# Expert slots of 384 tokens in place of 256, in the routed second layer of an attention and mixture kernel

## The chip, the core and the metric

The kernel runs on one core of a Trainium2 chip. Its engines work side by side, each through its own list of instructions in order: PE (TensorE, matrix products), DVE (VectorE) and ACT (ScalarE) for work on elements, POOL (GpSimd) for small work and for transfers whose addresses are computed on the chip, SP (SyncE) for the other transfers. They meet at semaphores. Matrix products land in PSUM, eight banks of 2 KB a partition, and ACT or DVE must read them out before a bank is used again. The metric is the device time of one execution in microseconds (us); runs of the same kernel are summed up by their median.

## The reference

Three stages follow each other. Windowed attention (4 sequences of 576, 8 heads of 64, each position sees the 64 up to itself) gives 2304 tokens of 512. A dense layer multiplies by `w_in` (512 x 2048), applies a clipped square and multiplies by `w_out`. A routed layer then sends each token to one of eight experts:

```python
logits = x @ w_gate + modality_bias[modality_id]
e_idx = np.argmax(logits, axis=1)
...
gate_w = probs[np.arange(N), e_idx]
for e in range(E):
    mask = e_idx == e
    h = np.maximum(x[mask] @ w1[e], 0.0)          # 512 -> 1024
    out[mask] = gate_w[mask, None] * (h @ w2[e])  # 1024 -> 512
```

With the inputs of the reference two experts get all tokens: 1136 and 1168 of 2304.

## The kernel before

**Precision by parts.** Every product of the dense and routed layers is made of three matrix products: each operand is split into a rounded part (made by ACT) and the rest (made by DVE), and high x high, low x high and high x low are added in PSUM. So a weight that is loaded costs an ACT cast and a DVE subtraction before PE can use it.

**The first two stages** go through the tokens in six chunks of 384 (`CT`). For each of 16 slices `f` of the hidden width, `l1` makes a tile of 128 x 384 with 12 matrix products (line 445), ACT and DVE turn it into two operands, and `l2` adds it into three banks of 128 x 512 (line 483). Attention of the next chunk is woven in. `route` (line 514) takes the logits of a finished chunk, picks experts, and scatters each token's number into tables by slot position (line 591). After the fourth chunk `order` puts the slots that are sure to be full in front, so that the first `EARLY` slots can begin before the last chunk is routed. `final` (line 663) ends the routing and writes the table `meta`, from which the later slots read their expert and their place.

**The routed layer** is a loop over `NS0` = 10 slots (lines 1071 to 1089). A slot is up to 256 (`SL`) tokens of one expert; a row of `SL` per slot is computed whether filled or not. Nine slots are whole; the tenth is a half slot (`half_slot`) of 128. Further slots stand under `tc.If(used > i)` and run only if the routing needs them.

- `gather` (line 748) runs on POOL: it reads the slot's token numbers and fetches the tokens, 128 at a time, from the stored output of the dense layer. `prep_half` (line 774) transposes 128 of them on PE (line 777) and splits them into `zh` and `zl` (ACT line 779, DVE line 780).
- `slot` (line 782), first layer: four PSUM tiles `hp` of 128 x 512, each holding two slices of 256 columns; 24 matrix products of 256 columns fill one (line 791). ACT writes the rounded relu (line 799), DVE the rest (line 800). Two PSUM buffers alternate, so a tile has to be read out while the next is filled.
- `l2_slot`, second layer: for each 128 tokens 24 matrix products of 512 columns (line 814), a scaled copy by ACT (line 821) and a scatter to the output by POOL (line 822).
- `wsteps` loads the expert weights of coming slots, 16 pieces of 256 KB a slot (line 722 on SP's queue), and splits each (ACT line 727, DVE line 728). Four buffers hold raw pieces, so the load of one begins when the piece four before it has been split. The table `PS` says how many of these steps stand behind each step of a slot: 3, 3, 3, 3 behind the four tiles of the first layer, then 2, 1, 1, 0.
- `advance` takes a step of the last chunk's `route`.

SP's order is that of the source throughout. ACT's is from the end of the dense layer on, and PE's from the third slot on. Elsewhere a scheduler of the language sets the order when the program is built.

Of the kernel before, what the change touches and what calls it, by code (L numbers as in the profile page):

```python
# [9 lines left out]
F32 = mybir.dt.float32  # L10
F32R = mybir.dt.float32r
# [6 lines left out]
P = 128  # L18
B, H, S, D = 4, 8, 576, 64
NT = B * S  # L20
# [50 lines left out]
def moe_kernel(ctx, tc, qT, kT, v, w_in, w_out, mod, wg, wgT, mbias, w1, w2, cst, tri, empty, out, spec):  # L71
# [113 lines left out]
        G.memset(t, 0.0)  # L185
        return t

    prod = tile_of([P, DM], "prod")
    wgb = []
    LGB = 4  # L190
    run = state([P, E], "run")
# [322 lines left out]
    def route(c):  # L514
# [16 lines left out]
        if c < NC - 1:  # L531
            store()
            lg = tile_of([P, TT, E], f"lgd{c}", tag="r_lg")
            for t in range(TT):
                for e in range(E):
                    V.tensor_tensor_reduce(  # L536
                        prod, yt[t], wgb[0][:, e, :], 1.0, 0.0, ALU.mult, ALU.add, lg[:, t, e : e + 1]
                    )
                    if e % LGB == LGB - 1:
                        yield  # L540
        else:
            lg = yield from pe_logits(c, yt)
            store()
# [74 lines left out]
            yield from final()  # L618

    def by_position(dst, vec, name):  # L620
        t = tile_of([P, NS, NS], name, tag="u", bufs=2)
        V.tensor_tensor(t, eqk, bc(vec, 1, NS), op=ALU.mult)
        V.tensor_reduce(dst, t, axis=AX.X, op=ALU.add)

# [120 lines left out]
    def w2s(i, f, lo):  # L745
        return piece(i % 2, (2 + lo) * NP + f)

    def gather(i, rows=NT, halves=2):
        rr = G.value_load(meta[0:1, 0 if i < KNOWN else 2, i : i + 1], min_val=0, max_val=(NS - 1) * SL)
        rt = tile_of([P, TT, 2, 2], f"rt{i}", tag="rt", bufs=2)  # L750
        for t in range(TT):
            G.dma_start(rt[:, t], tabs[t][bass.ds(rr, SL), :].rearrange("(h p) w -> p h w", p=P))
        rc = tile_of([P, 2, 2], f"rc{i}", tag="rc", bufs=4)
        oi = tile_of([P, 2], f"oi{i}", I32, tag="oi", bufs=4)
        gi = tile_of([P, 2], f"gi{i}", I32, tag="gi", bufs=4)
        gf = tile_of([P, 2], f"gf{i}", tag="gf", bufs=4)
# [12 lines left out]
        return g, oi, rc  # L769
# [37 lines left out]
    def l2_slot(i, g, t, mid):  # L807
        hh, hl = hid[0], hid[1]
        yo = ps.tile([P, DM], F32, tag=f"y{(2 * i + t) % TT}", name=f"yo{i}_{t}", bufs=1)
        n = 0  # L810
        sl = slice(t * P, (t + 1) * P)
        for f in range(NF2):
            for a, b in ((hh, 0), (hh, 1), (hl, 0)):
                T.matmul(yo, a[:, f, sl], w2s(i, f, b), start=n == 0, stop=n == 3 * NF2 - 1)  # L814
# [12 lines left out]

    def half_slot(i, g, x, mid):
        hh, hl = hid[0], hid[1]
        xh, xl = x  # L830
        sl = slice(0, HS)

        def l1(fp):
            hp = ps.tile([P, 2, P], F32, tag="h", name=f"hp{i}_{fp}", bufs=2)
            w = [experts[1, lo * NP // 2 + fp].rearrange("p (q k n) -> p k q n", q=2, k=KD) for lo in range(2)]
            n = 0
            for k in range(KD):
                for a, b in ((xh, 0), (xl, 0), (xh, 1)):
                    T.matmul(hp, a[:, k, sl], w[b][:, k], start=n == 0, stop=n == 3 * KD - 1)
                    n += 1  # L840
            r = tile_of([P, 2, P], f"hr{i}_{fp}", tag="y", bufs=4)
            A.activation(r, hp, AF.Relu)
            return r

        def turn(fp, r):
            rt = aux([P, 2, P], f"rt{i}_{fp}")
            for u in range(2):
                T.transpose(rt[:, u, :], r[:, u, :], C["ident"])
            fs = slice(2 * fp, 2 * fp + 2)
            A.copy(hh[:, fs, sl], rt)  # L850
            V.tensor_tensor(hl[:, fs, sl], rt, hh[:, fs, sl].bitcast(F32), op=ALU.subtract)
# [9 lines left out]
        yield from l2_slot(i, g, 0, mid)  # L861

    man = ExitStack()
    ET = mybir.EngineType
# [130 lines left out]
    for n in range(len(its) + LAG):  # L995
# [49 lines left out]
        if c == NC - 1 and f == 6:  # L1045
            ws = wsteps(0, NS0)
            eg = [gather(i, (NC - 1) * CT) for i in range(2)]
            ex = new_x2(0)
        if c == NC - 1 and f >= 9:
            for _ in range(2 if f < 11 or f == NF - 1 else 3):  # L1050
                next(ws)
                ndone += 1
            if f in (10, 11):
                prep_half(0, f - 10, eg[0], ex)
# [5 lines left out]
    hm = tile_of([P, 2, NF2, SL], "hm", F32R, tag="dec")  # L1060
    hid = [hm[:, 0], hm[:, 1]]
    gq = dict(enumerate(eg))
    gq[2] = gather(2, (NC - 1) * CT)
    x = ex
    PS = (3, 3, 3, 3, 2, 1, 1, 0)

    def advance():
        if rts and next(rts[0], "end") == "end":
            rts.clear()

    for i in range(NS0):
        if i == NS0 - 3:
            used = nc.values_load(nused[0:1, 0:1], min_val=1, max_val=NS + 1)  # L1073
        if i == 2:
            m2.enter_context(tc.manual_schedule(engines={ET.PE}))
        nx = new_x2(i + 1) if i + 1 < NS0 else None
        for n, _ in enumerate((slot if i + 1 < NS0 else half_slot)(i, gq[i], x, advance)):
            advance()
            for _ in range(PS[n]):
                next(ws, None)  # L1080
            if i == 0 and n == 3:
                gq[3] = gather(3, (NC - 1) * CT)
            if n == GN and EARLY <= i + GP < NS0:
                assert not rts
                gq[i + GP] = gather(i + GP, halves=2 if i + GP + 1 < NS0 else 1)
# [8 lines left out]
    for i in range(NS0, NS + 1):  # L1094
        ifs.enter_context(tc.If(used > i))
        g = gather(i)
        x = new_x2(i)
        for _ in wsteps(i, i + 1):
            pass
        for h in range(2):  # L1100
            prep_half(i, h, g, x)
        for _ in slot(i, g, x, lambda: None):
            pass
# [47 lines left out]
```

## Time and profile before

| | us |
|---|---|
| median of 3 runs (lowest, highest) | 747.73 (744.97, 749.30) |
| the profiled execution, its own time | 745.43 |
| its span from first to last instruction | 743.7 |
| PE busy in it | 731.2 |
| routed layer: first product to the half slot's start | 501.3 to 722.9 |
| half slot and last output | 722.9 to 743.7 |

All times in the rows are microseconds from the start of the span. A busy PE may still be short of its best rate: matrix products follow each other as a pipeline, and the length printed for one (284 ns) overlaps the next. The pace is the distance between two starts. What ended an idle time stands behind the arrow in a row.

### The profile page before, as it was taken

Reading aid. Unit: us, or ns where it says so; the run is one execution under the profiler, and the core shown is the slowest. Engines: PE = TensorE matmul, PEld = TensorE weight load, DVE = VectorE, ACT = ScalarE, POOL = GpSimd, SP = SyncE. Lnnn points to the kernel's source line nnn. Section 1 sums busy time; section 2 is a strip of 40 time slices with the busy share of each in tenths; the row PEclk is TensorE's granted clock in tenths of the full one; section 3 lists DMA queues with packets and bytes.
Section 4 is the critical chain, followed back from the end, with each engine's and each line's share of the span. In section 5 each row is a group of like instructions: output and inputs, shape, how many; then the busy total and the mean of one; then the engine's idle time right before and its main releaser. Section 6 shows DMA issues by size and latency. Waiting matters only on the chain. (4 is left out here: it accounts for less than half of the span.)

```text
span 743.7 us, 13351 instructions
## 1 busy us (share of the span) xinstructions
PE 731.2 (98%) x4456; PEld 623.2 (84%) x4456; DVE 497.2 (67%) x1479; ACT 417.1 (56%) x981; POOL 145.5 (20%) x219
## 2 busy tenths in 40 slices
PE   8999999999999999999999999999999999999995
PEld 5655557888999899888998899899888988999884
DVE  5998889984396538752696468857776565755530
ACT  6775679555555545554555445546546555655531
POOL 3200002112011200120110252061266342221110
PEclk9999999999999999999999999999999999999998
DMA  9886633123032203121310014147768667666520
GB/s 323 323 307 221 245 124 99 61 80 57 29 107 79 65 29 106 45 79 15 106 58 30 1 59 156 58 72 233 249 161 265 220 231 246 222 206 209 196 91 19
DMA packets 55774, 101.89 MB, mean 137 GB/s; under 512 B 8032, under 2 KB 17376, under 8 KB 55568
## 3 DMA queue, kind: packets, MB, share of 16 engines
q1 hardware_dynamic: 50976, 90.92, 37.4%
q0 software_dynamic: 4576, 9.79, 4.4%
q8 instruction: 37, 0.61, 0.3%
q14 instruction: 41, 0.34, 0.1%
q10 hardware_dynamic: 144, 0.24, 0.1%
HBM read 91.46 MB, written 9.84 MB: 136 GB/s over the span
## 5 line engine op out<-in xcount | busy, mean ns | idle before, releaser
L445 PE MATMUL h<-xh,w 128*128 128x384 f32 x640 | 180.4, 342 | 0.0
L483 PE MATMUL py<-w,gh 128*128 128x512 f32 x480 | 149.2, 394 | 0.0
L728 DVE TENSOR_TENSOR e<-wr,e 128x512 fp32r<-128x512 f32 x160 | 106.8, 688 | 47.0 <-ACT e L727 42.7
L727 ACT CAST e<-wr 128x512 fp32r<-128x512 f32 x160 | 96.9, 619 | 66.5 <-DMA wr<-in_w 65.1
L445 PEld LDWEIGHTS h<-xh,w 128*128 128x128 f32 x640 | 117.0, 188 | 4.5 <-DVE u L457 0.8
L814 PE MATMUL yo<-e,hm 128*128 128x512 f32 x456 | 112.0, 397 | 1.2 <-DVE hm L800 0.7
L448 ACT ACTIVATE u<-h,half 128x384 f32<-128x384 f32 x96 | 55.7, 580 | 99.0 <-PE h L445 74.9
L445 PE MATMUL h<-xl,w 128*128 128x384 f32 x320 | 108.0, 337 | 0.0
L791 PE MATMUL hp<-zh,e 128*128 128x256 f32 x576 | 106.5, 284 | 0.0
L814 PEld LDWEIGHTS yo<-e,hm 128*128 128x128 f32 x456 | 83.7, 188 | 20.5 <-DVE hm L800 1.6
L483 PEld LDWEIGHTS py<-w,gh 128*128 128x128 f32 x480 | 88.8, 188 | 13.9
L457 DVE SCALAR_TENSOR_TENSOR u<-u,h 128x384 f32<-128x384 f32 x80 | 44.2, 552 | 74.9 <-ACT u L449 69.2
L483 PE MATMUL py<-w,gl 128*128 128x512 f32 x240 | 93.1, 393 | 0.0
L791 PEld LDWEIGHTS hp<-zh,e 128*128 128x128 f32 x576 | 90.3, 190 | 0.6
L536 DVE CUSTOM_DVE_ANT_0 prod<-y,wgb 128x512 f32<-128x512 f32 x120 | 85.2, 710 | 0.9
L791 PE MATMUL hp<-zl,e 128*128 128x256 f32 x288 | 81.5, 283 | 0.0
L465 ACT CAST gh<-u 128x384 fp32r<-128x384 f32 x80 | 41.0, 512 | 61.6 <-PE py L483 33.3
L378 POOL TENSOR_TENSOR s<-s,sm 128x512 f32<-128x512 f32 (+1 forms) x24 | 26.9, 1120 | 239.5 <-DVE sm L368 93.9
L466 DVE TENSOR_TENSOR gl<-u,gh 128x384 fp32r<-128x384 f32 x80 | 45.3, 566 | 25.9 <-ACT gh L465 19.3
L445 PEld LDWEIGHTS h<-xl,w 128*128 128x128 f32 x320 | 60.2, 188 | 2.6 <-issue 0.2
L791 PEld LDWEIGHTS hp<-zl,e 128*128 128x128 f32 x288 | 54.8, 190 | 0.5
L355 ACT ACTIVATE s<-s,mx 128x128 f32<-128x128 f32 (+1 forms) x120 | 46.2, 388 | 15.3 <-DVE mx L345 15.3
(206 smaller groups left out, 1024.4 us busy)
## 6 DMA issues: line engine op xcount, KB each, us to landing
wr<-in_w SPq DMA_DIRECT2D x160, 256.0 KB
q<-in_qT SPq DMA_DIRECT2D x32, 256.0 KB
dec<-in_w_in SPq DMA_DIRECT2D x16, 512.0 KB
dec<-in_w_out SPq DMA_DIRECT2D x16, 512.0 KB
v<-in_v SPq DMA_DIRECT2D x27, 256.0 KB
k<-in_kT SPq DMA_DIRECT2D x15, 384.0 KB
yd<-y SPq DMA_DIRECT2D x18, 256.0 KB
wgb<-in_wgT SPq DMA_DIRECT2D x1, 2048.0 KB
```

Source lines behind the costliest of these rows:

```text
L355: A.activation(s[:, hp, :n], s[:, hp, :n], AF.Exp, bias=mx[:, hp : hp + 1], scale=-1.0, accum_out=sm[:, hp : hp + 1],)
L445: T.matmul(h, wi(f, a)[:, k, :], b[:, k, :], start=n == 0, stop=n == 3 * KD - 1)
L448: A.activation(u, h, AF.Relu, bias=half, scale=0.5)
L457: V.scalar_tensor_tensor(g, u, 1.0, h, op0=ALU.min, op1=ALU.max)
L465: A.copy(gh, u)
L466: V.tensor_tensor(gl, u, gh.bitcast(F32), op=ALU.subtract)
L483: T.matmul(ys[c][t], a[:, sl], wo(f, b), start=f == 0 and n == 0, stop=f == NF - 1 and n == 2)
L536: V.tensor_tensor_reduce(prod, yt[t], wgb[0][:, e, :], 1.0, 0.0, ALU.mult, ALU.add, lg[:, t, e : e + 1])
L727: A.copy(wpart(i, p, 0), t)
L728: V.tensor_tensor(wpart(i, p, 1), t, wpart(i, p, 0).bitcast(F32), op=ALU.subtract)
L791: T.matmul(hp[:, u, :], w1s(i, 2 * fp + u, k, a), b[:, k, :], start=n == 0, stop=n == 3 * KD - 1,)
L814: T.matmul(yo, a[:, f, sl], w2s(i, f, b), start=n == 0, stop=n == 3 * NF2 - 1)
```

## The change

- A slot is 384 tokens (`SL = CT`), in three parts of 128 (`SH`). `NS0` falls from 10 to 7: six whole slots and the half slot of 128, so the rows computed stay 2432. Three slots instead of four are early.
- The first layer makes eight PSUM tiles of 128 x 384 a slot, each with 12 products of 384 columns (line 791 of the new file), in place of four tiles with 24 products of 256. ACT's relu and DVE's rest are 384 wide. `advance` is no longer called between the halves of a tile.
- The rest `hl` lies partly in buffers that the dense layer has left (tags `gh`, `gl`, `u`). `prod`, a scratch of the routing, takes the place of `u` for `by_position`.
- The weights' steps are spread over 14 places a slot: `PS` is 1, 1, 2, 1, 1, 2, 1, 1 behind the tiles of the first layer and 1 behind each half of the second.
- POOL's order is fixed to the source from the sixth slot on; the register `used` is read there.
- The gathers of the first two slots stand two steps earlier in the source; the tables are a little narrower (16 slots at most, 20 before).

```diff
-SL = 256
-EARLY = 4
+SL = CT
+SH = SL // P
+EARLY = 3
 NS = (NT + E * (SL - 1)) // SL + EARLY
-NS0 = 10
+NS0 = 7
...
-        for h in range(halves):
-            t = tile_of([P, DM], f"g{i}_{h}", tag=("s", "k")[h], bufs=2)
+            t = tile_of([P, DM], f"g{i}_{h}", tag="ssk"[h], bufs=2)
...
     def slot(i, g, x, mid):
-        for fp in range(NF2 // 2):
-            hp = ps.tile([P, 2, SL], F32, tag="h", name=f"hp{i}_{fp}", bufs=2)
-            for u in range(2):
-                n = 0
-                for k in range(KD):
-                    for a, b in ((0, xh), (0, xl), (1, xh)):
-                        T.matmul(
-                            hp[:, u, :], w1s(i, 2 * fp + u, k, a), b[:, k, :],
-                            start=n == 0, stop=n == 3 * KD - 1,
-                        )
-                        n += 1
-                if u == 0:
-                    mid()
-            sl = slice(2 * fp, 2 * fp + 2)
-            A.activation(hh[:, sl, :], hp, AF.Relu)
-            V.scalar_tensor_tensor(
-                hl[:, sl, :], hp, 0.0, hh[:, sl, :].bitcast(F32), op0=ALU.max, op1=ALU.subtract
-            )
+        for f in range(NF2):
+            hp = ps.tile([P, SL], F32, tag="h", name=f"hp{i}_{f}", bufs=2)
+            n = 0
+            for k in range(KD):
+                for a, b in ((0, xh), (0, xl), (1, xh)):
+                    T.matmul(hp, w1s(i, f, k, a), b[:, k, :], start=n == 0, stop=n == 3 * KD - 1)
+                    n += 1
+            A.activation(hh[f], hp, AF.Relu)
+            V.scalar_tensor_tensor(hl[f], hp, 0.0, hh[f].bitcast(F32), op0=ALU.max, op1=ALU.subtract)
             yield
-        for t in range(2):
-            yield from l2_slot(i, g, t, mid)
+        for t in range(SH):
+            yield from l2_slot(i, g, t, mid, hid)
...
-    PS = (3, 3, 3, 3, 2, 1, 1, 0)
+    PS = (1, 1, 2, 1, 1, 2, 1, 1, 1, 1, 1, 1, 1, 1)
...
     for i in range(NS0):
-        if i == NS0 - 3:
+        if i == NS0 - 2:
+            m2.enter_context(tc.manual_schedule(engines={ET.Pool}))
             used = nc.values_load(nused[0:1, 0:1], min_val=1, max_val=NS + 1)
...
-            pn = 1 if i < EARLY - 1 else 4
-            if nx is not None and pn <= n < pn + (2 if i + 2 < NS0 else 1):
+            pn = 1 if i < EARLY - 1 else NF2
+            if nx is not None and pn <= n < pn + (SH if i + 2 < NS0 else 1):
```

Two places show what the change does to the engines that PE waits for. The first is ACT's list inside the first layer of a whole slot in the middle of the routed layer. `hp` are the PSUM tiles of the first layer, `hm` the relu's home, `wr` raw weight pieces and `e` their split form. Before:

```order
L799 ACTIVATE hm_5437<-hp6_0_7280 128x512
L727 CAST e1_3_5512<-wr7_6_7205 128x512
L727 CAST e1_3_5512<-wr7_7_7233 128x512
L727 CAST e1_8_5522<-wr7_8_7257 128x512
L799 ACTIVATE hm_5437<-hp6_1_7347 128x512
L727 CAST e1_8_5522<-wr7_9_7307 128x512
L727 CAST e1_9_5574<-wr7_10_7311 128x512
L727 CAST e1_9_5574<-wr7_11_7315 128x512
L799 ACTIVATE hm_5437<-hp6_2_7386 128x512
```

Now, ACT at the same place:

```order
L793 ACTIVATE hm_5451<-hp3_0_6596 128x384
L728 CAST e0_3_5241<-wr4_6_6552 128x512
L793 ACTIVATE hm_5451<-hp3_1_6645 128x384
L728 CAST e0_3_5241<-wr4_7_6569 128x512
L793 ACTIVATE hm_5451<-hp3_2_6664 128x384
L728 CAST e0_8_5281<-wr4_8_6590 128x512
L728 CAST e0_8_5281<-wr4_9_6611 128x512
L793 ACTIVATE hm_5451<-hp3_3_6687 128x384
```

Between two relus stood three casts; now one or two stand there, and the relus come twice as often.

The second place is DVE where the second slot begins. `fin`, `byp` and `meta` are the end of the routing (`final`), `hm<-hp1_0` is the rest of the second slot's first tile. Before:

```order
L585 CAST posi5_5772<-pos5_5708 128x3
L675 TENSOR_TENSOR finm_5834<-finm_5834,fin1_5826 128x160
L676 TENSOR_REDUCE fin3_5828<-finm_5834 128x20
L678 TENSOR_TENSOR fin3_5828<-fin3_5828,fin4_5829 128x20
L622 TENSOR_TENSOR byp4_5860<-eqk_106,fin3_5828 128x400
L800 SCALAR_TENSOR_TENSOR hm_5437<-hp1_0_5909,hm_5437 128x512
L728 TENSOR_TENSOR e0_7_5229<-wr2_6_5799,e0_3_5227 128x512
L623 TENSOR_REDUCE fin4_5829<-byp4_5860 128x20
```

Now, DVE at the same place:

```order
L700 TENSOR_SCALAR fin7_5833<-fin7_5833,fin2_5828 128x2x10
L701 TENSOR_TENSOR fin6_5832<-fin6_5832,fin7_5833 128x2x10
L729 TENSOR_TENSOR e0_6_5233<-wr2_5_5881,e0_2_5231 128x512
L702 TENSOR_SCALAR fin6_5832<-fin6_5832 128x17
L703 CAST meta_103<-fin6_5832 128x34
L794 SCALAR_TENSOR_TENSOR hm_5451<-hp1_0_5952,hm_5451 128x384
L729 TENSOR_TENSOR e0_7_5243<-wr2_6_5908,e0_3_5241 128x512
L794 SCALAR_TENSOR_TENSOR hm_5451<-hp1_1_5971,hm_5451 128x384
```

Before, the second slot's first tile was read out in the middle of `final`; now all of `final`, up to `meta`, stands ahead of it.

## Rows read from the trace of the kernel before

**Rows 1.** The page's part 1: busy us (share of the span) x instructions.

```profile
PE 731.2 (98%) x4456; PEld 623.2 (84%) x4456; DVE 497.2 (67%) x1479; ACT 417.1 (56%) x981; POOL 145.5 (20%) x219
```

**Rows 2.** Busy time by stretch: length, PE, PEld, DVE, ACT, POOL, PEclk, DMA share, GB/s.

```profile
500.00:550.00 50.00, 49.48 (x337) 44.82 (x335) 37.12 (x102) 27.55 (x51) 14.39 (x20) 1.00 0.65 205
550.00:600.00 50.00, 49.35 (x311) 43.96 (x312) 33.46 (x61) 30.47 (x54) 24.50 (x42) 1.00 0.73 239
```

**Rows 3.** Waits of PE from 440 on: us in total, times, longest.

```profile
PE yo L814 <- DVE hm L800: 0.7, 2, 0.5
PE yo L814 <- ACT hm L799: 0.4, 1, 0.4
```

**Rows 4.** Page's groups: line engine op out<-in xcount | busy, mean ns | idle before.

```profile
L728 DVE TENSOR_TENSOR e<-wr,e 128x512 fp32r<-128x512 f32 x160 | 106.8, 688 | 47.0 <-ACT e L727 42.7
L727 ACT CAST e<-wr 128x512 fp32r<-128x512 f32 x160 | 96.9, 619 | 66.5 <-DMA wr<-in_w 65.1
L814 PE MATMUL yo<-e,hm 128*128 128x512 f32 x456 | 112.0, 397 | 1.2 <-DVE hm L800 0.7
L448 ACT ACTIVATE u<-h,half 128x384 f32<-128x384 f32 x96 | 55.7, 580 | 99.0 <-PE h L445 74.9
L791 PE MATMUL hp<-zh,e 128*128 128x256 f32 x576 | 106.5, 284 | 0.0
L457 DVE SCALAR_TENSOR_TENSOR u<-u,h 128x384 f32<-128x384 f32 x80 | 44.2, 552 | 74.9 <-ACT u L449 69.2
L791 PE MATMUL hp<-zl,e 128*128 128x256 f32 x288 | 81.5, 283 | 0.0
```

**Rows 5.** Timeline of PE, start us, us, engine, line: a slot's whole first layer.

```profile
605.77 0.28 PE L791 MATMUL hp<-zh,e 128*128 128x256 f32 x1
...
617.27 2.93 PE L814 MATMUL yo<-e,hm 128*128 128x512 f32 x12
```

**Rows 6.** Timeline of PE: one tile of the dense layer, 12 products 384 wide.

```profile
492.96 0.34 PE L445 MATMUL h<-xh,w 128*128 128x384 f32 x1
...
495.07 0.63 PE L483 MATMUL py<-w,gh 128*128 128x512 f32 x2
```

**Rows 7.** Timeline of PE, ACT and DVE: a first-layer tile read out, ninth slot.

```profile
699.87 0.28 PE L791 MATMUL hp<-zh,e 128*128 128x256 f32 x1
...
702.92 0.60 ACT L799 ACTIVATE hm<-hp 128x512 fp32r<-128x512 f32 x1 [2.17 <-PE hp L791]
...
703.42 1.65 ACT L727 CAST e<-wr 128x512 fp32r<-128x512 f32 x3
703.56 0.69 DVE L800 SCALAR_TENSOR_TENSOR hm<-hp,hm 128x512 fp32r<-128x512 f32 x1 [4.54 <-ACT hm L799]
...
707.54 0.62 ACT L727 CAST e<-wr 128x512 fp32r<-128x512 f32 x1 [0.63 <-DMA wr<-in_w]
```

**Rows 8.** Timelines around 538 to 551: POOL, SP's queue, ACT, then PE.

```profile
538.12 0.98 POOL L591 DMA_INDIRECT tab<-rec,posi  x1 [1.47 <-DVE fin L676]
...
540.08 0.33 SPq L722 DMA_DIRECT2D wr<-in_w  x1
...
546.39 0.62 ACT L727 CAST e<-wr 128x512 fp32r<-128x512 f32 x1 [6.33 <-DMA wr<-in_w]
...
549.12 0.73 PE L814 MATMUL yo<-e,hm 128*128 128x512 f32 x2 [0.38 <-ACT hm L799]
550.34 7.71 PE L814 MATMUL yo<-e,hm 128*128 128x512 f32 x32 [0.48 <-DVE hm L800]
```

**Rows 9.** DVE from 531 to `meta`: all engines, then line 728's subtractions alone.

```profile
531.00:557.70 26.70, 25.84 (x162) 22.62 (x161) 21.63 (x78) 12.65 (x23) 14.41 (x20) 1.00 0.61 174
...
531.00:557.70 26.70, 10.14 (x16) 1.00 0.61 174
```

**Rows 10.** Timeline of ACT: the first slot's first relu; of PE: the half slot's start.

```profile
510.37 0.59 ACT L799 ACTIVATE hm<-hp 128x512 fp32r<-128x512 f32 x1
...
722.90 0.28 PE L839 MATMUL hp<-e,zh 128*128 128x256 f32 x1
```

More of the change, by code (lines that the diff above doesn't have):

```diff
@@ L186, in state @@
         return t
-    prod = tile_of([P, DM], "prod")
     wgb = []
@@ L620, in by_position @@
     def by_position(dst, vec, name):
-        t = tile_of([P, NS, NS], name, tag="u", bufs=2)
+        t = tile_of([P, NS, NS], name, tag="prod")
         V.tensor_tensor(t, eqk, bc(vec, 1, NS), op=ALU.mult)
@@ L746, in w2s, with gather @@
         return piece(i % 2, (2 + lo) * NP + f)
-    def gather(i, rows=NT, halves=2):
+    def gather(i, rows=NT, halves=SH):
         rr = G.value_load(meta[0:1, 0 if i < KNOWN else 2, i : i + 1], min_val=0, max_val=(NS - 1) * SL)
-        rt = tile_of([P, TT, 2, 2], f"rt{i}", tag="rt", bufs=2)
+        rt = tile_of([P, TT, SH, 2], f"rt{i}", tag="rt", bufs=2)
         for t in range(TT):
             G.dma_start(rt[:, t], tabs[t][bass.ds(rr, SL), :].rearrange("(h p) w -> p h w", p=P))
[L753 to L756, printed above, removed]
+        rc = tile_of([P, SH, 2], f"rc{i}", tag="rc", bufs=4)
+        oi = tile_of([P, SH], f"oi{i}", I32, tag="oi", bufs=4)
+        gi = tile_of([P, SH], f"gi{i}", I32, tag="gi", bufs=4)
+        gf = tile_of([P, SH], f"gf{i}", tag="gf", bufs=4)
         G.tensor_tensor(rc, rt[:, 0], rt[:, 1], op=ALU.add)
@@ L784, in slot, with l2_slot @@
         xh, xl = x
-        for fp in range(NF2 // 2):
-            hp = ps.tile([P, 2, SL], F32, tag="h", name=f"hp{i}_{fp}", bufs=2)
-            for u in range(2):
-                n = 0
-                for k in range(KD):
-                    for a, b in ((0, xh), (0, xl), (1, xh)):
-                        T.matmul(
-                            hp[:, u, :], w1s(i, 2 * fp + u, k, a), b[:, k, :],
-                            start=n == 0, stop=n == 3 * KD - 1,
-                        )
-                        n += 1
-                if u == 0:
-                    mid()
-            sl = slice(2 * fp, 2 * fp + 2)
-            A.activation(hh[:, sl, :], hp, AF.Relu)
-            V.scalar_tensor_tensor(
-                hl[:, sl, :], hp, 0.0, hh[:, sl, :].bitcast(F32), op0=ALU.max, op1=ALU.subtract
-            )
-            yield
-        for t in range(2):
-            yield from l2_slot(i, g, t, mid)
-    def l2_slot(i, g, t, mid):
-        hh, hl = hid[0], hid[1]
-        yo = ps.tile([P, DM], F32, tag=f"y{(2 * i + t) % TT}", name=f"yo{i}_{t}", bufs=1)
+        for f in range(NF2):
[7 more added lines that the diff above has]
+            V.scalar_tensor_tensor(hl[f], hp, 0.0, hh[f].bitcast(F32), op0=ALU.max, op1=ALU.subtract)
+            yield
+        for t in range(SH):
+            yield from l2_slot(i, g, t, mid, hid)
+    def l2_slot(i, g, t, mid, hid):
+        hh, hl = hid
+        yo = ps.tile([P, DM], F32, tag=f"y{t}", name=f"yo{i}_{t}", bufs=1)
         n = 0
@@ L813, in l2_slot @@
             for a, b in ((hh, 0), (hh, 1), (hl, 0)):
-                T.matmul(yo, a[:, f, sl], w2s(i, f, b), start=n == 0, stop=n == 3 * NF2 - 1)
+                T.matmul(yo, a[f][:, sl], w2s(i, f, b), start=n == 0, stop=n == 3 * NF2 - 1)
                 n += 1
@@ L828, in half_slot @@
     def half_slot(i, g, x, mid):
-        hh, hl = hid[0], hid[1]
+        hh, hl = (hm[:, u * NF2 * HS : (u + 1) * NF2 * HS].rearrange("p (f n) -> p f n", f=NF2) for u in range(2))
         xh, xl = x
@@ L834, in l1 @@
             hp = ps.tile([P, 2, P], F32, tag="h", name=f"hp{i}_{fp}", bufs=2)
-            w = [experts[1, lo * NP // 2 + fp].rearrange("p (q k n) -> p k q n", q=2, k=KD) for lo in range(2)]
+            w = [experts[i % 2, lo * NP // 2 + fp].rearrange("p (q k n) -> p k q n", q=2, k=KD) for lo in range(2)]
             n = 0
@@ L860, in half_slot @@
         turn(NF2 // 2 - 1, r)
-        yield from l2_slot(i, g, 0, mid)
+        yield from l2_slot(i, g, 0, mid, ([hh[:, f] for f in range(NF2)], [hl[:, f] for f in range(NF2)]))
     man = ExitStack()
@@ L1044, in moe_kernel @@
                 next(rts[0])
-        if c == NC - 1 and f == 6:
+        if c == NC - 1 and f == 4:
             ws = wsteps(0, NS0)
@@ L1052, in moe_kernel @@
                 ndone += 1
-            if f in (10, 11):
-                prep_half(0, f - 10, eg[0], ex)
+            if f in (9, 10, 11):
+                prep_half(0, f - 9, eg[0], ex)
         if c == NC:
@@ L1059, in moe_kernel @@
     assert ndone == 2 * NP + NLD + 6
-    hm = tile_of([P, 2, NF2, SL], "hm", F32R, tag="dec")
-    hid = [hm[:, 0], hm[:, 1]]
+    hm = tile_of([P, 4 * 2 * DM], "hm", F32R, tag="dec")
+    hid = [[hm[:, f * SL : (f + 1) * SL] for f in range(NF2)], [hm[:, f * SL : (f + 1) * SL] for f in range(NF2, NF2 + 2)]]
+    hid[1] += [tile_of([P, SL], f"hl{n}", F32R, tag=t, bufs=2) for n, t in enumerate(("gh", "gl", "gh", "gl", "u", "u"))]
     gq = dict(enumerate(eg))
@@ L1080, in moe_kernel @@
                 next(ws, None)
-            if i == 0 and n == 3:
-                gq[3] = gather(3, (NC - 1) * CT)
             if n == GN and EARLY <= i + GP < NS0:
                 assert not rts
-                gq[i + GP] = gather(i + GP, halves=2 if i + GP + 1 < NS0 else 1)
-            pn = 1 if i < EARLY - 1 else 4
-            if nx is not None and pn <= n < pn + (2 if i + 2 < NS0 else 1):
+                gq[i + GP] = gather(i + GP, halves=SH if i + GP + 1 < NS0 else 1)
+            pn = 1 if i < EARLY - 1 else NF2
+            if nx is not None and pn <= n < pn + (SH if i + 2 < NS0 else 1):
                 prep_half(i + 1, n - pn, gq[i + 1], nx)
@@ L1099, in moe_kernel @@
             pass
-        for h in range(2):
+        for h in range(SH):
             prep_half(i, h, g, x)
```

5 lines of the change are left out of this document (3 added, 2 removed).

## The prediction, made before the changed kernel was run

> **What bounds the kernel now.** I read the busy shares first: PE is busy in 731.2 of 743.7 us [rows 1], so any time that is won has to be PE's. Then the stretches of the routed layer: in the two that hold its first three slots PE falls short of full by 0.5 and 0.65 us [rows 2], and the waits of PE from 440 on name 0.7 and 0.4 us that end with the read-out of first-layer tiles (`hm`) [rows 3]. The DMA engines, ACT and DVE are half to two thirds busy, and the long idle times of ACT and DVE before line 727 and line 728 (66.5 and 47.0 us) are waits for weights that PE never felt [rows 4]. So I count PE's products, then look for places where PE begins to wait. The sum is made against the profiled execution, 745.43 us (1.7 outside its span); the median of the runs is 2.3 higher, and the predicted time is that median plus my sum.
>
> **What the first layer costs.** Before, nine whole slots have 96 products of 256 columns, 864 in all (576 and 288) [rows 4]. One slot's 96 start at 605.77 and give way at 617.27 [rows 5]: 11.50 / 96 = 0.1198 us each, 103.5 us for 864. After, six slots have 96 products of 384, 576 in all. The dense layer shows that shape: 12 products from 492.96 to 495.07 [rows 6], 2.11 / 12 = 0.1758 us each, 101.3 us for 576. The gain is **2.2 us**. The columns are the same in number (221,184), so what is saved is the part of a product's time that doesn't grow with its columns: between the two shapes 128 columns more cost 0.056 us, which leaves 0.0078 of 0.1198 as fixed, and 288 products fewer save 288 x 0.0078 = 2.2. Bounds: if the slots' own slower surroundings made 384 columns cost in proportion (0.1797), nothing would be saved; if the pace fell to 0.173 (less than the 0.1758 of rows 6 by what two starts there can be misread), 3.8.
>
> The Trainium skill, page "TensorE: Matmul & The Clock Gate", section "Back-to-back issue gap", speaks against even this gain: it puts a lone product's gap at the columns over 2.4 GHz plus 2.5 ns. By it 288 products fewer would save 288 x 2.5 ns = 0.7 us, an estimate; the rows' paces lie 13 and 16 ns above columns over clock, and the measurement decides.
>
> **What stays.** The second layer keeps 19 parts of 24 products (456) [rows 4], and as many tokens are transposed. The half slot starts at 722.90 [rows 10] and takes 20.8 us to the end, as before: it has the same shape, and its weights come sooner in its predecessor. Zero for all three.
>
> **What goes.** 48 of 160 loads of 256 KB, each with a cast of 0.619 and a subtraction of 0.688 [rows 4]: 30 us of ACT, 33 of DVE, 12.6 MB. All of it lies under PE's work, so it is worth nothing by itself. It is cover against waits: a slot now takes about 96 x 0.1758 + 72 x 0.236 = 34 us for 16 pieces, where it took 11.5 + 48 x 0.236 = 23 (0.236 from rows 8, below).
>
> **The read-out of tiles.** This is the step with the least margin. A tile is now filled in 2.11 us instead of 2.88 (24 x 0.1198), and with two buffers it must be read out while the next is filled. In rows 7 the tile begun at 699.87 is full at 702.75; the relu starts at 702.92 and takes 0.60, the rest starts at 703.56. With 384 columns they take 0.580 and 0.552 [rows 4]: read out about 0.17 + 0.58 + 0.04 + 0.55 = 1.35, say 1.5 with the signal to PE, so 0.6 us of play. ACT has 0.58 + 0.62 or 0.58 + 1.24 to do per tile, DVE 0.55 + 0.69 or 0.55 + 1.38; both fit 2.11. I take zero, and price the failure below.
>
> **The waits of the first slots.** The two waits of 0.38 and 0.48 us behind the second slot's tiles have a cause in rows 8: POOL scatters the last chunk's slot positions at 538.12, a weight load issued at 540.08 is not cast before 546.39, ACT sits 6.33 us in front of that cast, and the relu of a tile is queued behind it. The event stays in the program. What changes is what PE has in hand: by then only the second layer of the first slot. DVE's new order puts all of `final` ahead of the second slot's first tile. I bound that: from 531 to `meta` DVE was busy 21.6 us, 10.1 of it with 16 weight pieces [rows 9], so the routing with some tiles was at most 11.5; now 8 pieces stand in that stretch, 5.1, so at most 16.6 in all. PE's cover from the last rank product to the place where that tile's buffer is needed again is 55 second-layer products at 0.236 (7.71 less the last one's 0.39, over 31 [rows 4, 8]), three first-layer tiles at 2.11 and 12 transposes at 0.11: about 20.6. So 4 us are spare, and DVE's idle time in the old stretch was 26.7 - 21.6 = 5.1. The wait lies between 0 and about 2; nearer 0, as the bound counts tiles in: 0.3. One more at the start of the first slot: PE reaches the first second-layer product after 24 + 18 products and 12 transposes, at about 501.3 + 4.2 + 4.1 + 1.3 = 510.9, and the relu that it needs ended at 510.96 [rows 10]; with the dense layer's last banks copied 0.7 later, I put 0.3, between 0 and 1. So 1.1 us of old waits go and 0.6 come: **-0.5**.
>
> **POOL.** The fourth slot's gather needs `meta`, written before at 557.7 at the latest (the end of the stretch in rows 9) and now ahead of the second slot's first read-out, and its tokens are transposed first inside the third slot's second layer, near 590. That leaves over 30 us for ten small steps and three fetches: nothing. The fixed order of POOL from the sixth slot on keeps each output scatter behind one fetch whose buffer comes free in that slot's second layer: nothing.
>
> **Sum: -2.2 - 0.5 = -2.7 us**, 0.4%; 742.7 for a profiled execution like the one before, **745.0** for the median.
>
> **The rivals.**
> 1. Cleaner than that: the pace is 0.173 and no wait is left, -3.8 - 1.1 = -4.9, 742.8. For it: ACT and DVE have a third less weight work per token. Against: rows 6. Just beyond 0.5%.
> 2. A fixed part of only 2.5 ns per product (the rule above): -0.7 - 0.5 = -1.2, 746.5. By rows 5 and 6 unlikely.
> 3. Slower, through the read-out: where two casts stand between relus (`PS` = 2, twice a slot), one tile later is read out late if casts also wait for weights, as at 707.54 for 0.63 us [rows 7]. ACT then needs 0.58 + 2 x (0.62 + 0.63) = 3.1 for a period of 2.11; 0.6 of that is play, 0.4 is lost. If every such tile and its successor lose it, 24 x 0.4 = 9.6: -2.7 + 9.6 = +6.9, 754.6. It decides once a relu starts more than 0.8 us after its tile is full. Against it: the loads have on average 2.1 us each in place of 1.46.
> 4. The change doesn't compute in seven slots: the routing asks for an eighth under `tc.If`. It would run alone, some 34 us of products and 16 loads in front: +50, 798. With 1136 and 1168 tokens three and four slots of 384 hold all, and the last has 16 tokens, fewer than the 128 of the half slot; only other inputs would do it.
>
> **How the numbers follow.** Forecast 0.58, rival 1 0.17, rival 2 0.09, rival 3 0.13, rival 4 with any other failure of order 0.03. A measurement of this kernel can tell about 0.5% (3.7 us, so 744.0 and 751.5) from no change. The forecast's own bounds (gain of products 0 to 3.8, waits -1.1 to +1.9) run from 742.8 to 749.6; 0.05 of its chance lies under 744.0 and 0.01 above 751.5. So faster 0.22, slower 0.17, same 0.61. The range from 742.0 to 750.5 takes in rivals 1 and 2 and the forecast's bounds and leaves out most of 3 and 4.
>
> **What would show it.** Right: 12 first-layer products in 2.1 us; a slot 33 to 34 us long in the middle; no idle of PE before line 791 in slots three to six; idle of PE under 1 us where the second slot begins; the half slot still 20.8 us from the end. Wrong: idle before line 791 that ends with DVE's line 794 (rival 3), a slower pace than 0.1758 beside the same DMA traffic, or work under `tc.If`.

## The result, and the profile after

The changed kernel takes **739.62 us** (median of six, 739.02 to 740.22) beside 747.01 for the kernel before on the same chip (six, 744.47 to 749.30): a ratio of **0.9905** [0.9883, 0.9927]. It is faster by 7.4 us where 2.7 were forecast, and lies below the stated range. Its times spread over 1.2 us, those of before over 4.8. The profiled executions are 745.43 and 739.57 us long, 5.9 apart.

PE is still busy in all but 12 us. The page's part 1 of the changed kernel (beside [rows 1]):

```profile
PE 725.8 (98%) x4168; PEld 619.5 (84%) x4168; DVE 465.5 (63%) x1442; ACT 388.6 (53%) x945; POOL 130.2 (18%) x189
```

Busy time by stretch, changed kernel (columns as in [rows 2]):

```profile
500.00:550.00 50.00, 50.00 (x282) 45.68 (x282) 34.74 (x108) 23.18 (x46) 9.28 (x9) 1.00 0.55 162
550.00:600.00 50.00, 50.00 (x262) 45.99 (x261) 27.99 (x47) 25.15 (x49) 24.56 (x41) 1.00 0.61 195
```

The 0.5 and 0.65 us that PE lacked in [rows 2] are gone, and the list of PE's waits holds none for `hm` any more. The event behind them is still there: a scatter of the last chunk, a weight cast that comes late, a relu queued behind it. Timeline of POOL, changed kernel (columns as in [rows 5], to be read beside [rows 8]):

```profile
538.32 1.02 POOL L592 DMA_INDIRECT tab<-rec,posi  x1 [17.63 <-DVE finm L676]
```

And of ACT:

```profile
548.27 0.62 ACT L728 CAST e<-wr 128x512 fp32r<-128x512 f32 x1 [3.23 <-DMA wr<-in_w]
548.80 0.48 ACT L793 ACTIVATE hm<-hp 128x384 fp32r<-128x384 f32 x1
```

ACT waits 3.23 us for that load instead of 6.33, and PE had the first slot's longer second layer in hand. (That the scatter is what makes the load late is an argument from the order of these rows; no run here moved the scatter.) A whole slot in the middle, timeline of PE, changed kernel:

```profile
578.90 0.33 PE L791 MATMUL hp<-zh,e 128*128 128x384 f32 x1
...
595.57 0.63 PE L806 MATMUL yo<-e,hm 128*128 128x512 f32 x2
...
613.39 0.33 PE L791 MATMUL hp<-zh,e 128*128 128x384 f32 x1
...
722.90 5.72 PE L806 MATMUL yo<-e,hm 128*128 128x512 f32 x24
```

The 96 first-layer products start within 16.67 us, 0.1736 us each, and a slot is 34.5 us long. The last row is the half slot's second layer: the same 24 products that took 5.82 us in the kernel before.

**Where the 5.9 us of the profiles lie.** I summed the distance from each product's start to the next one's, by the line of the first of the two; a wait counts to the product before it.

| | before, us | after, us | |
|---|---|---|---|
| first layer, 864 and 576 products | 104.05 | 100.63 | -3.4 |
| second layer, 455 distances | 108.96 | 105.48 | -3.5 |
| start (line 330, first loads) | 35.54 | 34.89 | -0.6 |
| last product to the end | 8.3 | 9.5 | +1.2 |

The dense layer's two lines differ by under 0.4. So the first layer brought more than forecast, the second layer, put at zero besides its waits, brought most of the rest, and the end took 1.2 back. The start is no part of the change: over all the profiles here it lies between 34.7 and 36.2 us.

### The profile page after: what moved, and what is told of

It reads as the page before. It is cut to its first block, busy times and chain, and to the rows that moved or that the text cites. A ratio compares the mean times of both kernels' runs of the same rounds, so it can differ in the third digit from the quotient of the medians.

```text
span 737.7 us, 12420 instructions
## 1 busy us (share of the span) xinstructions
PE 725.8 (98%) x4168; PEld 619.5 (84%) x4168; DVE 465.5 (63%) x1442; ACT 388.6 (53%) x945; POOL 130.2 (18%) x189
## 5 line engine op out<-in xcount | busy, mean ns | idle before, releaser
L729 DVE TENSOR_TENSOR e<-wr,e 128x512 fp32r<-128x512 f32 x112 | 74.5, 688 | 44.7 <-ACT e L728 40.6
L791 PE MATMUL hp<-zh,e 128*128 128x384 f32 x384 | 101.0, 336 | 0.0
L806 PE MATMUL yo<-e,hm 128*128 128x512 f32 x348 | 99.0, 394 | 0.0
L806 PEld LDWEIGHTS yo<-e,hm 128*128 128x128 f32 x348 | 64.2, 188 | 12.4
L728 ACT CAST e<-wr 128x512 fp32r<-128x512 f32 x112 | 66.0, 616 | 15.5 <-DMA wr<-in_w 15.4
L791 PEld LDWEIGHTS hp<-zh,e 128*128 128x128 f32 x384 | 69.6, 188 | 1.1 <-DVE hm L794 0.4
L791 PE MATMUL hp<-zl,e 128*128 128x384 f32 x192 | 64.3, 335 | 0.0
L483 PEld LDWEIGHTS py<-w,gl 128*128 128x128 f32 x240 | 45.0, 188 | 9.5
```

The lines of the kernel that those rows point to most:

```text
L483: T.matmul(ys[c][t], a[:, sl], wo(f, b), start=f == 0 and n == 0, stop=f == NF - 1 and n == 2)
L728: A.copy(wpart(i, p, 0), t)
L729: V.tensor_tensor(wpart(i, p, 1), t, wpart(i, p, 0).bitcast(F32), op=ALU.subtract)
L791: T.matmul(hp, w1s(i, f, k, a), b[:, k, :], start=n == 0, stop=n == 3 * KD - 1)
L806: T.matmul(yo, a[f][:, sl], w2s(i, f, b), start=n == 0, stop=n == 3 * NF2 - 1)
```

## Experiments

Three theories of the second layer: **traffic** (weight loads, casts and subtractions slow the products, and there are fewer now), **place** (the hidden values have cells of 384 now), **rhythm** (the pace is what PE ran ahead of it). A fourth, **addresses** (where in memory a product's two operands lie: the stationary one, which is loaded ahead of it, and the moving one, which streams through), came out of the first runs.

**The kernel before, once more.** No edit.

> The kernel before, unchanged, for a second profile. The change gained 6.0 us of span between the two profiles, of which 3.4 lie in the first layer (0.1204 to 0.1747 us a product, 864 to 576 of them), 3.5 in the second (455 distances, mean 0.2395 to 0.2318, median 0.232 to 0.227). If the second layer's pace is a property of the program, its median is 0.231 to 0.233 again and the first layer's 0.120. If it is chance from execution to execution, the median comes out elsewhere, down to 0.227. The six times of this kernel spread over 4.8 us (744.5 to 749.3) where those of the changed one spread over 1.2; if the waits of PE at the second slot (1.1 us in the first profile) are what varies, another profile shows another sum there.

Measured: 747.9 us (one run), 2.5 more than the first profiled execution. Second-layer median 0.232, first layer 104.05 us again: the pace belongs to the program. The wait does not. Timeline of PE in this execution:

```profile
550.23 0.74 PE L814 MATMUL yo<-e,hm 128*128 128x512 f32 x2 [1.83 <-ACT hm L799]
551.45 9.28 PE L814 MATMUL yo<-e,hm 128*128 128x512 f32 x32 [0.48 <-DVE hm L800]
```

Busy time by stretch right behind it:

```profile
552.00:554.00 2.00, 2.00 (x7) 1.55 (x6) 1.00 (x4) 1.40 (x3) 1.01 (x2) 0.58 0.70 229
554.00:556.00 2.00, 2.00 (x7) 1.56 (x6) 2.00 (x6) 1.85 (x4) 1.33 (x6) 0.57 0.58 162
```

The wait is 2.3 us instead of 0.86 at the same two tiles [rows 8], and after it the granted clock is 0.57 to 0.58 for four microseconds, most of them at the lower of its two levels (1.2 GHz): seven products take 427 ns each, and the same 32 products take 9.28 us, where [rows 8] has 7.71. So the longer wait cost twice in this execution, and the first profile showed a mild case of it. A wait of that length doesn't always slow the clock, as the next run shows.

**Only the cells.** The kernel before with hidden values in cells of 384, and, since the old buffers `u` hold some of them, the routing's scratch in `prod`.

```diff
-        t = tile_of([P, NS, NS], name, tag="u", bufs=2)
+        t = prod[:, : NS * NS].rearrange("p (a b) -> p a b", a=NS)
...
-    hm = tile_of([P, 2, NF2, SL], "hm", F32R, tag="dec")
...
+    cells = hm[:, : (NF2 + 2) * CT].rearrange("p (f n) -> p f n", n=CT)
...
```

> The kernel before (slots of 256, its four tiles of 2 x 256, its weights), with only the home of the hidden values as in the change: cells 384 wide of which 256 are used, the rest of the relu in the dense layer's old buffers. The subtraction that writes it is two instructions of 256 instead of one of 512. Place theory (the second layer is faster because the hidden values lie elsewhere): median distance of second-layer products 0.227 instead of 0.232, the second layer 2 to 2.5 us shorter, 742.5 to 745. Rhythm theory (the pace follows from what PE ran ahead of it, products of 256 columns) and traffic theory (weight loads, casts and subtractions beside it): 0.231 to 0.233 as before, time as before within 0.3%.

Measured: 746.5 us, 0.9985 [0.9969, 1.0001]. The median is 0.227, but PE waits 2.9 us for `hm` and `hl`. Timeline of PE at the longest of these waits, and busy time by stretch behind it:

```profile
550.77 0.73 PE L817 MATMUL yo<-e,hm 128*128 128x512 f32 x2 [2.20 <-ACT hm L799]
```
```profile
552.00:554.00 2.00, 2.00 (x10) 1.62 (x10) 1.43 (x4) 1.01 (x2) 2.00 (x4) 1.00 0.54 178
```

The granted clock stays at 1.00 (the higher level, 2.4 GHz) here, behind a wait longer than the 1.83 us of the run above. The dense layer's starts, which have no part in the cells, also took on the changed kernel's pattern. So the cells are not the only candidate: the first edit of the diff shown makes `u` 64 bytes shorter (1600 to 1536) and moves what lies behind the two buffers by 128.

**No weights from the third slot on.**

```diff
-            if n < len(q):
+            if n < len(q) and not 2 <= q[n][0] < NS0:
-            if n >= NLD:
+            if n >= NLD and not 2 <= q[n - NLD][0] < NS0:
```

> The kernel before, but the weights of slots 2 to 9 are neither loaded nor split: those slots multiply with the weights of the first two slots, which lie in the same buffers. So from about 560 us on the 256 KB loads, ACT's casts and DVE's subtractions are gone. Traffic theory: the second-layer median falls from 0.232 to 0.227 and the first layer's from 0.120 to 0.117, together 5 us from there on, about 741. Place and rhythm theories: 0.231 to 0.233 and 0.120 as before; only waits can go, at most the 1.1 us at the second slot, so 745 to 747.5.

Measured: 743.17 us, 0.9939 [0.9919, 0.9960], spread 1.1 us. Second-layer median 0.231, first layer 104.04 us: the pace doesn't see the traffic. The Trainium skill says as much of the transfers (page "SBUF — State Buffer", section "SBUF: two separate sides": transfers and engines use separate ports and can't contend). But 5.1 us are gone, where the profile of before had 1.1 us of waits to lose. The list of PE's waits of this run has no `hm` at all:

```profile
PE warm L883 <- DVE wz L880: 1.3, 1, 1.3
PE sc L330 <- DMA lent<-in_qT: 0.8, 1, 0.8
PE rt L848 <- ACT hr L842: 0.3, 1, 0.3
```

**48 weight pieces back in the changed kernel.**

```diff
...
-        q = [(i, p) for i in range(first, last) for p in range(2 * NP)]
+        q = [(i, p) for i in range(first, last) for p in range(2 * NP) for _ in range(2 if 0 < i < NS0 and p % 2 else 1)]
...
-    PS = (1, 1, 2, 1, 1, 2, 1, 1, 1, 1, 1, 1, 1, 1)
+    PS = (1, 2, 2, 2, 2, 2, 2, 2, 2, 1, 2, 1, 1, 1)
```

> The changed kernel with 48 more weight pieces: in slots 1 to 6 every other piece is loaded and split twice, so that the 160 loads of 256 KB, casts and subtractions of the kernel before are back; the table of steps is raised to hold them. Traffic theory: the second-layer median goes back from 0.227 to 0.231 or more and the first layer's from 0.173 to 0.176, +3 to +4 us, 743 to 744. Place and rhythm theories: 0.227 and 0.173 stay, and the time stays at 739.6 but for waits. The rival of the prediction that was about read-out (two casts between relus, a relu that comes more than 0.8 us late) would show here if anywhere: idle of PE before line 791 that ends with the relu or the subtraction, 0.4 us each time, up to +10.

Measured: 763.1 us, 1.0206 [1.0161, 1.0252], some 23 us over the changed kernel. Medians 0.227 and 0.174: no pace moved, and the traffic theory is done. All of it is waiting, and slow products after waits. PE's waits of this run:

```profile
PE hp L791 <- DVE hl L794: 6.0, 5, 2.4
PE yo L806 <- ACT hm L793: 4.8, 2, 4.3
PE hp L791 <- DVE hm L794: 4.2, 2, 3.7
```

Its timeline of PE at the second slot:

```profile
556.09 1.47 PE L806 MATMUL yo<-e,hm 128*128 128x512 f32 x3 [4.30 <-ACT hm L793]
```

Its timeline of ACT ahead of that, a late cast and then the relu:

```profile
553.29 0.62 ACT L728 CAST e<-wr 128x512 fp32r<-128x512 f32 x1 [2.44 <-DMA wr<-in_w]
...
555.55 0.48 ACT L793 ACTIVATE hm<-hp 128x384 fp32r<-128x384 f32 x1
```

And its busy time in two stretches behind a later wait, of 3.69 us:

```profile
594.86:598.00 3.14, 3.14 (x10) 3.14 (x11) 2.20 (x4) 1.91 (x4) 2.15 (x7) 0.50 0.84 279
598.00:600.50 2.50, 2.50 (x10) 2.50 (x9) 1.22 (x3) 1.00 (x2) 0.39 (x1) 0.50 0.68 226
```

This is the prediction's third rival, a relu behind casts whose loads come late, with the loads put back. (The doubled pieces also share their raw buffers unevenly, so the size is this kernel's own.) The slots of 384 alone don't remove the wait at the second slot; with the loads of before it is 4.3 us long.

**Only the scratch.** The edit of the scratch (`prod` in place of `u`) by itself, in the kernel before.

> The kernel before (slots of 256, hidden values as before) with one side effect of the change alone: the routing's scratch of 1600 bytes lies in prod and no longer in the buffers u, which shrink from 1600 to 1536 bytes each, so that every buffer behind the two moves by 128 bytes. In the profiles before, products whose stationary and moving operand lie at the same address modulo 256 bytes settle at 173.4 ns (384 columns) and 226.8 (512), those that lie 128 apart at 175.8 and 231.7 to 232.5; nearly all second-layer products of the routed layer were 128 apart, here none is. Address theory: median of the second layer 0.227, 2 us less than before, 744.5 to 746.5 by the median, ratio 0.997. Place theory (it is the 384-wide cells that matter): 0.232 and time as before.

Measured: 747.24 us, 0.9991 [0.9976, 1.0006], median 0.227: the address theory's pace with the place theory's time. The half slot's row in the timeline of PE:

```profile
733.25 5.72 PE L814 MATMUL yo<-e,hm 128*128 128x512 f32 x24
```

PE's waits of this run:

```profile
PE yo L814 <- ACT hm L799: 3.0, 3, 1.4
PE yo L814 <- DVE hm L800: 0.7, 2, 0.5
PE hp L791 <- DVE zl L780: 0.5, 1, 0.5
PE hp L791 <- DVE hm L800: 0.2, 1, 0.2
```

The 24 products take 5.72 us with the cells of before. In this execution PE waits away what it gains, 4.4 us; it is 1.5 us above the median of this kernel, so the waits are a long sample.

**The changed kernel with its addresses moved.** Buffers `u` longer by 64, 128 and 32 bytes, so that what lies behind the two moves by 128, 256 and 64:

```diff
-        u = tile_of([P, CT], f"u{c}_{f}", tag="u", bufs=2)
+        u = tile_of([P, CT + 16], f"u{c}_{f}", tag="u", bufs=2)[:, :CT]
```

> The changed kernel with buffers u 64 bytes longer (1600 bytes, unused), so that every buffer behind the two lies 128 bytes further, as before the change. Address theory: the second layer of the routed layer goes back to a median of 0.231 or 0.232, half of the dense layer's first layer to 0.1758, time +2 to +3 us, 741.5 to 743; the routed first layer stays at 0.173. Place theory: 0.227, time as the changed kernel (739.6).

> The changed kernel with buffers u 128 bytes longer, so that what lies behind moves by 256 bytes. Address theory: only the difference modulo 256 counts, so pace and time as the changed kernel: median 0.227, 739.6. If any shift from the changed kernel's addresses hurts, it is slower by the 2 to 3 us of the 128-byte shift.

> The changed kernel with buffers u 32 bytes longer, so that what lies behind moves by 64 bytes: stationary and moving operands of the routed second layer 64 apart modulo 256. If 64 apart is as good as 0 (only whole 128s count), median 0.227; if every difference other than 0 costs alike, 0.231 to 0.232; in between is possible too.

Measured: 741.07 us (0.9906 [0.9885, 0.9927]), 740.5 (0.9898 [0.9870, 0.9925]) and 741.1 (one run). The half slot's 24 products, in this order, one row of each run:

```profile
725.37 5.80 PE L806 MATMUL yo<-e,hm 128*128 128x512 f32 x24
```
```profile
723.94 5.73 PE L806 MATMUL yo<-e,hm 128*128 128x512 f32 x24
```
```profile
724.37 5.78 PE L806 MATMUL yo<-e,hm 128*128 128x512 f32 x24
```

The routed second layer has medians of 0.232, 0.228 and 0.231 and sums of 107.04, 105.98 and 106.59 us (105.48 in the changed kernel). So the address theory holds for the pace: a shift of 128 brings the old pace back, one of 256 doesn't, one of 64 lies between. By the distances it is worth 1.1 to 1.6 us. In time the two medians lie 0.6 us apart (741.07 and 740.5) and their intervals overlap, so no gain in time is shown; the 2 to 3 that I expected were too many. Nor does the pace pay everywhere: as the programs were built, 360 of the 720 products of the dense layer's line 483 (512 columns) had operands 128 apart before and none after, yet the 720 took 167.22 us before and 167.57 after.

**128 bytes ahead of the large buffers.** The changed kernel and, beside it on the same chip, the same with a buffer of 128 bytes in front.

> The changed kernel once more, beside the others on the same chip: 739.5 to 741, second layer's median 0.227, first layer's 0.173, no wait of PE for hm or hl. If its six close times (1.2 us apart) were luck, a wait at the second slot and a wider spread show here.

> The changed kernel with 128 unused bytes ahead of the large buffers: stationary and moving operands of nearly all products now both lie at 0 modulo 256 instead of both at 128. If only their difference counts, pace and time are those of the changed kernel. If the place itself counts too, the settled pace (0.1734, 0.2267) stays or the start of each run of products (the first ten second-layer products take 229, 233, 236, 224, 231, 236, 229, 232, 231 ns) is shorter: up to 0.04 us for each of some 200 runs of products in the dense and routed layers, so up to 5 us faster.

Measured: 741.36 us (0.9899 [0.9879, 0.9918]) and 740.13 (0.9890 [0.9870, 0.9910]); both have median 0.227, a second-layer sum of 105.75 and the same starts of runs. For the second layer, then, only the difference of the two addresses counts. The first of these profiles has two waits for `hm`, of 0.25 us at the second slot and 0.29 at the third, so the changed kernel isn't wholly free of them. The two times can't be told apart, and no kernel tried here beats the changed one beyond that.

**Weight steps late, caught up at once.** In the kernel before, no weight step from the first slot's second layer to the second slot's third tile; without and with the scratch in `prod`.

```diff
+    LATE = {0: (3, 3, 3, 3, 0, 0, 0, 0), 1: (0, 0, 0, 3, 4, 3, 3, 3), 2: (4, 4, 3, 3, 2, 1, 1, 2)}
-            for _ in range(PS[n]):
+            for _ in range(LATE.get(i, PS)[n]):
```

> The kernel before with twelve weight steps moved: no load or split is issued from the second layer of the first slot to the third tile of the second slot, and they are caught up later in the second and third slots. So the relus of the second slot's first three tiles no longer stand on ACT behind a cast whose load came late through the scatter of the last chunk (in four profiles of slots of 256 PE waited 1.1, 2.3, 2.9 and 3.7 us there for the second slot's tiles; in the profile without those loads, 0). Wait theory (the 1.1 us of the first profile were a lucky sample, the kernel before usually loses 3 to 5 us there): ratio 0.994 to 0.996, some 743.5 to 745.5 beside 748 of before on the same chip, spread as small as in the run without weights (1.1 us); no wait of PE for hm between 540 and 560; paces as before (0.232, 0.120). Rival: the extra of the median over the first profile is elsewhere (start, tail); then at most the 1.1 us go, ratio 0.998 to 1.

> The kernel before with both: the twelve weight steps late, and the routing's scratch in prod so that operands lie at the same address modulo 256. Theory: the change's gain is the sum of three things, waits at the second slot, addresses of the second layer, and fewer products in the first layer. Then this kernel has the first two (second-layer median 0.227, no wait at the second slot) and stands 1.5 to 2 us below the run with the steps late alone, and the changed kernel stands another 3 to 4 us below this one (3.4 by the first layer's distances, 104.05 to 100.63). Rival (the rest of the gain is something else in the change, such as the order of GpSimd or the fewer weight loads): the distance left to the changed kernel is far from 3.4.

Measured: 752.56 us (1.0059 [1.0043, 1.0074]) and 753.01 (1.0062 [1.0046, 1.0078]). Both expectations fell. Timeline of PE in the first of them:

```profile
565.93 0.58 PE L791 MATMUL hp<-zh,e 128*128 128x256 f32 x1 [3.48 <-DVE hm L800]
572.10 0.38 PE L791 MATMUL hp<-zh,e 128*128 128x256 f32 x1 [1.15 <-DVE hm L800]
580.73 0.73 PE L814 MATMUL yo<-e,hm 128*128 128x512 f32 x2 [1.03 <-ACT hm L799]
```

The second slot's first read-outs came on time and the wait went to the third slot, where the pieces are caught up: beside the 16 that a slot of 23 us loads anyway, the loads came too late.

**Weight steps late, caught up slowly.** Six steps late, one more a slot after that; without and with the scratch in `prod`.

```diff
+    LATE = {0: (3, 3, 3, 3, 0, 0, 0, 0), 1: (0, 1, 3, 3, 2, 2, 2, 1)}
+    LATE.update({i: (3, 3, 3, 3, 2, 1, 1, 1) for i in range(2, 8)})
```

> The kernel before with six weight steps late, caught up one a slot over slots 2 to 7 (the run with twelve late steps, caught up within two slots, had no wait at the second slot's first tiles but 5.9 us at the third slot's, behind casts whose loads came late, and was 0.6% slower). Wait theory: no wait of PE for hm at the second slot, under 1 us at the third, ratio to before 0.994 to 0.997. Rival: the kernel of 256 has no room for late loads anywhere (16 loads in 23 us), the wait moves again and the ratio is 0.998 or more.

> The same with the routing's scratch in prod, so that both operands lie at the same address modulo 256: second-layer median 0.227 where the run beside it has 0.232, 1.5 to 2 us below it. If waits and addresses are the first two parts of the gain and the first layer's fewer products the third, the changed kernel (0.9895 of before) stands 3 to 4 us below this one. Rival: the pace gained is given back in waits, as where the scratch alone was moved (ratio 0.9991).

Measured: **744.28 us, 0.9957** [0.9938, 0.9975], and **743.61 us, 0.9949** [0.9931, 0.9968]. Timeline of ACT in the first of them, two relus of the second slot:

```profile
542.55 0.60 ACT L799 ACTIVATE hm<-hp 128x512 fp32r<-128x512 f32 x1 [1.27 <-PE hp L791]
...
545.38 0.60 ACT L799 ACTIVATE hm<-hp 128x512 fp32r<-128x512 f32 x1 [0.19 <-PE hp L791]
```

PE's one wait for a read-out in it:

```profile
566.57 0.39 PE L791 MATMUL hp<-zh,e 128*128 128x256 f32 x1 [0.81 <-DVE hm L800]
```

The relus wait for PE now, not for a cast. So the kernel before loses some 0.43% in that place, **3.2 us** of 747.35 (1.9 to 4.6), where its first profile showed 1.1; with the later weights left out it was 5.1, and here 0.81 us of waiting is left. With the addresses alike the second layer's sum falls from 107.62 to 106.49, and 0.7 us of time follow (the intervals overlap). From there to the changed kernel (0.9905 and 0.9899) 0.44 to 0.50% are left, 3.3 to 3.7 us: the size of the first layer's 3.4. That is not a clean test of it. The profile of the second kernel (1.7 us above its median) has some 2.2 us of waits for `hm`, `zh` and `zl` that the changed kernel's first profile doesn't have, and the changed kernel's end is 1.2 us longer: two terms of opposite sign that no run separates. The first layer's 3.4 rests on the distances.

## Why the prediction was wrong, point by point

| part | forecast | measured |
|---|---|---|
| waits of the second slot | -1.1 old, +0.6 new | -3.2 (1.9 to 4.6), +0 to 0.5 |
| first layer | -2.2 (0 to -3.8) | -3.4 |
| second layer's pace | 0 | -1.1 to -1.6 by distances, not clear of the noise in time |
| the end | 0 | +1.2 |
| sum | -2.7 | -7.4 |

**The waits, the largest miss.** "So 1.1 us of old waits go": the place was right, and so was the relu queued behind a late cast [rows 3, 8]; the size came from one mild execution. Even there the idle time was less than the cost: the products around the two waits start 0.77, 0.34, 0.88 and 0.34 us apart, 1.4 us more than four at 0.232, for 0.86 us of idle time. The text itself says that the median lies 2.3 us above the profiled time, and carries those 2.3 over as if they belonged to the kernel as a whole. Most of them belonged to this wait: the second profile has it at 2.3 us with 1.6 us of half-speed products behind it, and the run with the weight steps spread gives back 3.2, about 1.1 plus the 2.3 (3.4). The new waits of 0.6 hardly came: none for a read-out in the first profile of the changed kernel and in the four with its addresses moved, 0.54 in the second, half of it at the third slot, for which none was forecast.

**The first layer.** The step that failed is the price of 384 columns, 0.1758 from [rows 6], and the fixed part of 7.8 ns that follows; the slots' 96 products took 0.1736 each. Settled products of 256, 384 and 512 columns follow each other at 120.0, 173.4 and 226.8 ns: columns at 2.4 GHz (the granted clock is 1.00) plus 13.3. 288 x 13.3 = 3.8; slower starts of runs leave 3.4. Rows 6 show a run of 12 products, which is too short to show the settled pace whatever the addresses. In the kernel before that tile had its weights 128 bytes off its moving operand, and from the third on its products take 174 to 178 ns to the end. In the changed kernel the two lie alike, and the tile takes 2.11 us all the same. Timeline of PE, changed kernel:

```profile
492.83 0.33 PE L445 MATMUL h<-xh,w 128*128 128x384 f32 x1
...
494.94 0.63 PE L483 MATMUL py<-w,gh 128*128 128x512 f32 x2
```

Its first six products take 171, 175, 177, 185, 176 and 182 ns, the others 173. So the pace of a run of 12 was set beside that of a run of 96, and their difference was taken for a law. The 2.5 ns of the Trainium skill (page "TensorE: Matmul & The Clock Gate", section "Back-to-back issue gap"), an estimate of 0.7 us, is further off: the measurement decides.

**"What stays: zero".** The second layer's pace moved through a line of the diff that I read as a matter of space, the scratch that went from `u` to `prod`. The end was put at zero too, and is 1.2 us longer (below).

**"Worth nothing by itself".** The 48 pieces less are a part of what keeps the wait small: put back, they cost some 23 us, in a kernel of their own arrangement; the loads taken out of the kernel before give 5.1. I took them for cover, and didn't see that the cover had run out in usual executions.

**Right.** Next to no wait for read-outs in the slots of 384 (0.29 us, at the third slot, in one profile), slots of 34.5 us (34), the first second-layer product at 510.79 (510.9), nothing from POOL or `meta`, no work under `tc.If`. Rival 1 named the direction and both its sources, and was still 3 us short. The end is 1.2 us longer: 8.7 to 9.7 us from the last product to the end in the seven profiles of slots of 384, 8.1 to 9.0 in the nine of 256. In the two first profiles all of it lies behind POOL's last scatter, whose end is 5.4 us before the end of the span in the kernel before and 6.6 in the changed one. Why was not tried. With it the parts of the table make 6.0 to 7.0 us; what is missing to 7.4 is well within what the waits are known to (1.9 to 4.6).

## What to carry over

A profile is one execution. Where the median lies well above it and the times spread, look for the wait in that profile which could be longer in others, and price it by the spread, and not by the one sample. A pace is only transferable between two places when the runs of products are of like length and the operands lie alike in both: compare both before a few nanoseconds become a law. And a step "under cover" is worth what it keeps from becoming late.

## What the runs showed of the hardware

- **Addresses of a product's two operands.** Settled distances (seventh product of a run on), by the difference of the addresses of stationary and moving operand modulo 256 bytes, addresses as the program was built: 0 gives 173.4 ns (384 columns) and 226.8 to 227.7 (512); 128 gives 175.8 and 231.7 to 232.5; 64 gives 175.2 and 230.6. With one shift of both by 128 the second layer's pace doesn't change. Runs of nine products are too short for it: in the changed kernel the dense layer's products of 512 columns, all with a difference of 0, are still at 228, 232 and 231 ns (medians) in their seventh to ninth. The Trainium skill (page "SBUF — State Buffer", section "Who interferes with whom") gives PE two independent read ports, one for the moving operand and one for weights; these distances show that the two are not quite without effect on each other. What in the chip does it was not tried.
- **Starts of runs.** In the changed kernel the first products after a switch between shapes are slower: 229, 234, 235, 225, 230, 236, 229, 232, 231 ns before 512 columns settle at 227; 171, 175, 178, 185, 176, 181 before 384 settle at 173. Not every switch does this: with the addresses moved by 128 a slot's first layer begins at 174, 174, 175, 174 and 173.
- **The clock after a wait.** After waits of 0.38 and 0.48 us the granted clock stayed at 1.00 (2.4 GHz); after 1.83 and 0.48 it was 0.57 to 0.58 for 4 us; after 3.7 us it was 0.50 (1.2 GHz) for 5.6 us, products of 384 columns 320 ns apart. But after 2.20 and 0.22 us, at the same place of the program, it stayed at 1.00: the length of the wait alone doesn't decide it.
